# One adaLN block on one core: condition and beta loaded as single rows and spread by TensorE, and half of the second segment's LayerNorm statistics moved to an earlier place

## The chip, the cores and the metric

The kernel runs on one core of one Trainium2 chip. The metric is the device time of one execution in microseconds (us), the median of several executions. The engines are TensorE (PE in the profile, with its weight loads as PEld), VectorE (DVE), ScalarE (ACT), GpSimd (POOL) and SyncE (SP), which issues nearly all DMAs here.

## The reference

The block is a conditioned transformer layer on x of 2048 rows by 512 columns, all in float32. Six vectors of 512 come from a condition vector `c` of 512. The attention half runs over four segments of 512 rows with 32 heads of 16 columns; each segment attends within itself, and a compressed memory `M`, `z` carries what came before. A gate per head, `g = sigmoid(beta)`, mixes the two. The second half is a bilinear feed-forward part of 1376 columns.

```python
mod = (_silu(c) @ w_mod).reshape(c.shape[0], 6, 1, -1)
sa, ca, ga, sb, cb, gb = (mod[:, 0], mod[:, 1], mod[:, 2], mod[:, 3], mod[:, 4], mod[:, 5])
h = _layernorm(x, axis=-1) * (1 + ca) + sa
x = x + ga * _A_ref(h, A_wq, A_wk, A_wv, A_wo, A_beta)
h = _layernorm(x, axis=-1) * (1 + cb) + sb
x = x + gb * _B_ref(h, B_w_gate, B_w_up, B_w_down)
...
o = g * a_mem + (1.0 - g) * a_dot
M = M + jnp.einsum("bhld,bhle->bhde", pk, vs)
```

## The kernel before, in words

**The opening.** The kernel first needs two of the six vectors, `sa` and `ca`, as columns. SP's queue issues the loads in this order: four tiles of `x` for segment 0 (128 x 512 each), the first half of the needed columns of `w_mod` (tiles `wm`, four loads of 256 KB), the first weights of k (`wrk`), the second half of `wm`, the weights of q (`wrq`) and of v (`wrv`), and then those of k and q for the heads' groups 1 and 2. ScalarE's queue issues two small loads: `c` as a tile `s_c` of 128 partitions x 4 (L628), and `beta` sent to all 128 partitions as `be`, 128 x 32 (L669). While these travel, TensorE multiplies a tile of zeros (`wu`) 18 times (L658, `NWU = 18`, output `wups`, never read).

From `s_c` ScalarE and VectorE make silu(c): `e1 = exp(-c)`, plus one, reciprocal, product (L670 to L673). TensorE then multiplies by the first half of `wm` (`mod0(0)`, tile `m` in the profile). VectorE meanwhile takes mean and variance of the four tiles of `x` (`bn_stats` and `bn_aggr`, tiles `ast` and `amv`) and normalises them; TensorE transposes them (tiles `atp`), multiplies by the second half of `wm` (`mod0(1)`, whose first operand, `r0[1][1]`, is prepared by ScalarE and VectorE), and goes on to the projections k, q (`kps`, `qps`) and v (`vps`). VectorE's and ScalarE's work here is held in the order of the text by two chains, `CV` and `CA`; TensorE's by `pe()`.

**The gates.** `gates()` (L677 to L690) turns `be` into `gg` (from `exp(-beta)`) and `omg` (from `exp(beta)`): one VectorE step on each, a copy of `omg` into the eight `v` tiles by GpSimd, then the two reciprocals on VectorE, and products with a mask `hmg` on GpSimd.

**The loop.** 32 units follow (four segments, four groups of eight heads, two halves), each with five slots. In each slot the code, written out by hand, places the products for the row maxima (`q_half`: TensorE product `q<-kst,qst`, then VectorE's maximum over it, one custom instruction that reads PSUM and a short one that reads out `nm`), the logits and exponentials (`k_step`), and the sums over v (`av_step`). Between them `fill()` hands out pieces of the other work from a generator `fill_a`: projections of the next groups, the memory's steps, and the LayerNorm of the next segment (`ln`, which yields after each tile's statistics). `weave(a, b, at)` lets pieces of `b` follow the pieces of `a` whose numbers stand in `at`. For segment 1 the loads of `x` (`xload`, L643) and the LayerNorm begin in `fill_a` at segment 0, group 2: its four statistics go into the pieces 0, 1, 2, 3 of `Q`, the projection of q.

**Staging.** `staged()` hands out the tiles that raw weights are loaded into; four of them have the tag `x`, that is, they use the same four buffers as the tiles of `x`.

Of the kernel before, what the change touches and what calls it, by code (L numbers as in the profile page):

```python
# [57 lines left out]
def tile_kernel(ctx, tc, x, wq, wk_, wv, wo, beta, w_gate, w_up, w_down, c, w_mod, out):  # L58
# [113 lines left out]
    def ln(pool, hpool, xt, s, sc, sh, pfx, hb, fast):  # L172

        first = pfx == "a" and s == 0
        V, A = (CV, CA) if first else (vec, act)
        mv = pool.tile([P, 4, 2], F32, tag="mv", name=f"{pfx}mv{s}", bufs=2)
        for t in range(4):
            st = pool.tile([P, 6], F32, tag="st", name=f"{pfx}st{s}_{t}", bufs=2)
            i = V.bn_stats(st, xt[t])
            if not first:  # L180
                pin(i)
            V.bn_aggr(mv[:, t, :], st)
            if not first:
                yield 0.0
        sd = pool.tile([P, 4], F32, tag="sd", name=f"{pfx}sd{s}", bufs=2)
        A.activation(sd, mv[:, :, 1], AF.Ln, bias=epst[:, 0:1])
        y = pool.tile([P, 4], F32, tag="y", name=f"{pfx}y{s}", bufs=2)
        A.activation(y, sd, AF.Exp, scale=-0.5)
        a = pool.tile([P, 4], F32, tag="ya", name=f"{pfx}ya{s}", bufs=2)
        b = pool.tile([P, 4], F32, tag="yb", name=f"{pfx}yb{s}", bufs=2)  # L190
        eng = CV if first else nc.gpsimd
        eng.tensor_mul(a, y, y)
        if first:
            CV.scalar_tensor_tensor(b, mv[:, :, 1], EPS, a, op0=ALU.add, op1=ALU.mult)
        else:
            eng.tensor_scalar(b, mv[:, :, 1], 1.0, EPS, op0=ALU.mult, op1=ALU.add)
            eng.tensor_mul(b, b, a)
        eng.tensor_scalar(b, b, -0.5, 1.5, op0=ALU.mult, op1=ALU.add)
        eng.tensor_mul(y, y, b)
        yield 0.0  # L200
        tps = [bank(f"{pfx}tp{s}_{d}") for d in range(KT)] if first else []
        for t in range(4):
            i = V.tensor_scalar(xt[t], xt[t], mv[:, t, 0:1], y[:, t:t + 1],
                                op0=ALU.subtract, op1=ALU.mult)
            if not first:
                pin(i)
                yield 0.0
            for d, ps in enumerate(tps):
                TP(ps[:, t * P:(t + 1) * P], xt[t][:, d * P:(d + 1) * P], ident)
        if first:  # L210
            yield 0.0
        hH, hL = [], []
        if first:
            hcur[0] = hH, hL
        for d in range(KT):
            if first:
                ps = tps[d]
            else:
                ps = bank(f"{pfx}tp{s}_{d}", small=pfx == "c" and s == 0)
                for t in range(4):  # L220
                    TP(ps[:, t * P:(t + 1) * P], xt[t][:, d * P:(d + 1) * P], ident)
            h = pool.tile([P, L], F32, tag="hf", name=f"{pfx}hf{s}_{d}", bufs=hb[2])
            A.activation(h, ps, AF.Identity, scale=sc[:, d:d + 1], bias=sh[:, d:d + 1])
            hi = hpool.tile([P, L], F32R, tag=hb[0].format(d), name=f"{pfx}hH{s}_{d}", bufs=hb[1])
            lo = hpool.tile([P, L], F32R, tag=hb[0].format(4 + d), name=f"{pfx}hL{s}_{d}", bufs=hb[1])
            if fast:
                if d % 2:
                    A.activation(hi, h, AF.Copy)
                else:
                    V.tensor_copy(hi, h)  # L230
                V.tensor_sub(lo, h, hi.bitcast(F32))
# [393 lines left out]

    pwpool, pw = open_pool(name="pw", bufs=1, reuse_waits="tile")
    papool, pa = open_pool(name="pa", bufs=2, reuse_waits="tile")
    nc.scalar.dma_start(s_c, c)  # L628
    wm = w_mod.rearrange("(k p) n -> p k n", p=P)

    def load_mod(i):
# [13 lines left out]
        return xt  # L645

    xts = {0: xload(0)}
    NWU = 18
    wu = pa.tile([P, 512], BF, tag="rl", name="wu", bufs=1)
    vec.memset(wu, 0.0)  # L650
    wups = psp.tile([P, 2, 512], F32, tag="lk", name="wups", bufs=1)
# [2 lines left out]
        for i in range(n):  # L654
            MM(wups[:, 0], wu[:, 0:P], wu, start=True, stop=True)

    warm(NWU)
    wm0 = []  # L658
    for k in range(KT):
        a = ap.tile([P, 2, 2, 256], F32, tag="pt", name=f"wm0_{k}", bufs=PT)  # L660
# [5 lines left out]

    wm0_load(0)
    r0 = [[a[:, j].rearrange("p i c -> p (i c)") for a in wm0] for j in range(2)]
    nc.scalar.dma_start(be, beta[None, :].to_broadcast([P, H]))  # L669
    act.activation(e1, s_c, AF.Exp, scale=-1.0)  # L670
    CV.tensor_scalar_add(e1, e1, 1.0)
    CV.reciprocal(e1, e1)
    scl = CV.tensor_mul(s_c, s_c, e1)  # L673
    for a in kst:
        tc.add_manual_dep(nc.gpsimd.memset(a[96:98].rearrange("p h t -> p (h t)").bitcast(F32), ONES2).ins, scl.ins.name, SYNC, reason="order")

    def gates():  # L677

        CA.activation(gg, be, AF.Exp, scale=-1.0)
        act.activation(omg, be, AF.Exp)  # L680
        CV.tensor_scalar(omg, omg, 1e30, 1.0, op0=ALU.min, op1=ALU.add)
        for a in vt[0] + vt[1]:
            nc.gpsimd.tensor_copy(a[:, 0:H * VS].rearrange("p (h e) -> p h e", e=VS)[:, :, DH], omg)
        CV.tensor_scalar_add(gg, gg, 1.0)
        for tl in (gg, omg):
            CV.reciprocal(tl, tl)
        for g in range(NG):
            nc.gpsimd.tensor_mul(hmg[:, g, :, 0:DH], hmg[:, g, :, 0:DH],
                                 gg[:, g * HG:(g + 1) * HG].unsqueeze(2).to_broadcast([P, HG, DH]))
            nc.gpsimd.tensor_mul(hmg[:, g, :, DH], hmg[:, g, :, DH], omg[:, g * HG:(g + 1) * HG])  # L690
# [51 lines left out]
                i += 1  # L742

    wH, wL = {}, {}
    stage = [("ph", 3), ("ph", 3), ("ph", 3), ("mem", 1), ("pkr", 1), ("f", 2)] + [("x", 4)] * 4 + [("mem", 1), ("memb", 2)]
    nst = [0]

    def staged(nm):
        tg, n = stage[nst[0] % len(stage)]
        nst[0] += 1  # L750
        return (ap if tg == "memb" else pa).tile([P, D], F32, tag=tg, name=f"wr{nm}", bufs=n)

    def load_g(nm, w, g):
# [223 lines left out]
    def fill_a():  # L977
# [1 line left out]
            next(w)  # L979
        yield from av  # L980
        memq.extend((a_mem(0, 0), a_mem(0, 1)))
        lns = None
        for s in range(NSEG):
            if s > 0:
                hcur[0] = yield from lns
# [2 lines left out]
            for g in range(2 if s == 0 else 0, NG):  # L988
# [7 lines left out]
                    B["orl"] = wo_load(0, wpool)  # L996
                if g >= 2 and s + 1 < NSEG:
                    if g == 2:
                        xts[s + 1] = xload(s + 1)
                        lns = a_ln(s + 1)  # L1000
                        Q = weave(Q, lns, (0, 1, 2, 3))
                    else:
                        K = weave(K, lns, (1,) if s > 0 else (0, 1, 3))
                        Q = weave(Q, lns, (0, 1, 2, 3) if s > 0 else (0, 1))
# [125 lines left out]
    w1 = [load_g(nm, w, 1) for nm, w in (("k", wk_), ("q", wq))]  # L1130
    for w in w1:
        next(w)
    run(kq0[1])
    run(kq0[0])
    load(0)
# [4 lines left out]
        next(w)  # L1140
    for i in range(3):
        next(av)
    gates()
    w2 = [load_g(nm, w, 2) for nm, w in (("k", wk_), ("q", wq))]
    for w in w2:
# [536 lines left out]
```

## Time and profile before

| | |
|---|---|
| median of three runs | 854.2 us (853.75 to 854.21) |
| the profiled execution's own time | 854.15 us |
| its span, first to last instruction | 852.4 us |
| PE busy | 835.3 us, 98% of the span |
| DVE busy | 643.1 us, 75% |
| ACT busy | 499.0 us, 59% |
| POOL busy | 276.8 us, 32% |
| granted TensorE clock of the run | 1.0 |

All times in the text count from the span's start. A row of the timeline has the start, the time, the engine, the line, the operation, the tiles (output before the arrow), the shapes and a count; in brackets stands the engine's idle time before it and what the profile infers to have ended it. Rows of one engine with the same line and tiles that follow each other are merged, with a count. VectorE's operations through the chain `CV` all have line L39, and TensorE's through its helper L85 or L88, so they are told apart by their tiles.

### The profile page before, as it was taken

Reading aid. Unit: us, or ns where it says so; the run is one execution under the profiler, and the core shown is the slowest. Engines: PE = TensorE matmul, PEld = TensorE weight load, DVE = VectorE, ACT = ScalarE, POOL = GpSimd, SP = SyncE. Lnnn points to the kernel's source line nnn. Section 1 sums busy time; section 2 is a strip of 40 time slices with the busy share of each in tenths; the row PEclk is TensorE's granted clock in tenths of the full one; section 3 lists DMA queues with packets and bytes.
Section 4 is the critical chain, followed back from the end, with each engine's and each line's share of the span. In section 5 each row is a group of like instructions: output and inputs, shape, how many; then the busy total and the mean of one; then the engine's idle time right before and its main releaser. Section 6 shows DMA issues by size and latency. Waiting matters only on the chain.

```text
span 852.4 us, 14404 instructions
## 1 busy us (share of the span) xinstructions
PE 835.3 (98%) x4972; PEld 597.4 (70%) x4972; DVE 643.1 (75%) x1797; ACT 499.0 (59%) x760; POOL 276.8 (32%) x423
## 2 busy tenths in 40 slices
PE   9989999999999999999999999999999999999998
PEld 6756656666665656666665687888888778888886
DVE  7897768887778967787888359989987855447654
ACT  4758767787676876677545626344435555555330
POOL 2756627566565774675434610000000000000000
PEclk9999999999999999999999999999999999999999
DMA  9645435563545554466675466587650685335102
GB/s 271 155 152 155 121 104 141 158 179 115 143 106 166 144 165 106 122 170 213 195 216 155 145 192 230 189 287 271 253 201 28 234 271 210 121 135 184 43 8 98
DMA packets 83928, 139.57 MB, mean 164 GB/s; under 512 B 12720, under 2 KB 46768, under 8 KB 83856
## 3 DMA queue, kind: packets, MB, share of 16 engines
q1 hardware_dynamic: 83424, 138.51, 52.0%
q8 instruction: 39, 0.64, 0.3%
q14 instruction: 33, 0.27, 0.1%
q10 hardware_dynamic: 432, 0.15, 0.1%
HBM read 89.87 MB, written 48.50 MB: 162 GB/s over the span
## 4 chain that ended last, share of the span: by engine, by line
PE 61%; DVE 5%; ACT 1%; issue 0%; POOL 0%; DVEq 0%
PE acc L1358 14%; PE Xg L1289 7%; PE Xu L1289 6%; PE wops L85 5%; PE tb L85 5%; PE Yu L1289 4%; PE Yg L1289 4%; PE k L85 3%; PE q L85 3%; DVE q L39 2%; PE Zg L1289 1%; PE Zu L1289 1%; PE qps L85 1%; PE vps L85 1%; PE Xx L1289 1%; PE up L85 1%
## 5 line engine op out<-in xcount | busy, mean ns | idle before, releaser
L39 DVE CUSTOM_DVE_ANT_0 q<-q,cmask 128x384 f32<-128x384 f32 (+3 forms) x512 | 248.2, 503 | 71.1 <-PE q L85 63.5
L335 ACT ACTIVATE pt<-k 128x1024 f32<-128x1024 f32 x160 | 164.0, 1025 | 74.2 <-PE k L85 71.4
L341 POOL TENSOR_SCALAR_AFFINE_SELECT pt<-pt 128x256 f32<-128x256 f32 (+1 forms) x224 | 98.0, 452 | 137.2 <-ACT pt L335 136.9
L85 PE MATMUL q<-kst,qst 96*128 96x384 bf16 (+3 forms) x512 | 122.8, 302 | 6.5 <-DVE nm L39 5.1
L85 PE MATMUL k<-qst,kst 98*128 98x384 bf16 (+3 forms) x512 | 96.0, 299 | 1.6 <-ACT pt L335 1.3
L1366 DVE TENSOR_TENSOR xa<-xa,acc 128x512 f32<-128x512 f32 x95 | 64.9, 684 | 39.6 <-PE acc L1358 37.8
L85 PEld LDWEIGHTS <-qst 96*128 96x128 bf16 x512 | 43.9, 98 | 58.4 <-issue 43.6
L85 PE MATMUL tb<-pt,v 128*32 128x512 f32 (+3 forms) x1024 | 75.5, 436 | 0.0
L39 DVE DVE_READ_ACCUMULATOR2_ANT nm<- 128x1 f32 x512 | 71.8, 140 | 0.0
L85 PEld LDWEIGHTS <-kst 98*128 98x128 bf16 x512 | 44.4, 98 | 24.9 <-issue 8.8
L1358 PE MATMUL acc<-dH,mH 128*128 128x512 f32 (+1 forms) x152 | 60.3, 397 | 0.0
L1358 PE MATMUL acc<-dL,mH 128*128 128x512 f32 (+1 forms) x152 | 60.1, 395 | 0.0
L1358 PE MATMUL acc<-dH,mL 128*128 128x512 f32 (+1 forms) x152 | 60.0, 395 | 0.0
L85 PEld LDWEIGHTS tb<-pt,v 128*32 128x32 f32 x1024 | 28.7, 109 | 38.6 <-issue 35.7
L367 ACT ACTIVATE tsb<-tb 128x512 f32<-128x512 f32 x32 | 19.1, 596 | 31.6 <-PE tb L85 31.5
L1358 PEld LDWEIGHTS acc<-dH,mL 128*128 128x128 f32 (+1 forms) x152 | 28.5, 188 | 7.1 <-DVE mL L1309 0.3
L1358 PEld LDWEIGHTS acc<-dL,mH 128*128 128x128 f32 (+1 forms) x152 | 28.6, 188 | 7.0
L1358 PEld LDWEIGHTS acc<-dH,mH 128*128 128x128 f32 (+1 forms) x152 | 28.5, 188 | 6.8
L85 PE MATMUL kps<-ahH,wkH 128*128 128x512 f32 x64 | 29.4, 460 | 0.0
L85 PE MATMUL qps<-ahH,wqH 128*128 128x512 f32 x64 | 28.7, 448 | 0.2 <-DVE oL L39 0.2
L85 PE MATMUL vps<-wvH,ahH 128*128 128x512 f32 x64 | 28.3, 442 | 0.0
L85 PE MATMUL wops<-woH,oH 128*128 128x512 f32 x64 | 28.3, 442 | 0.0
(403 smaller groups left out, 2019.1 us busy)
## 6 DMA issues: line engine op xcount, KB each, us to landing
wm<-in_w_mod_dram SPq DMA_DIRECT2D x24, 256.0 KB, 3.9
kd<-k SPq DMA_DIRECT2D x16, 384.0 KB, 2.5
qd<-q SPq DMA_DIRECT2D x16, 384.0 KB, 3.5
kst<-kd SPq DMA_DIRECT2D x32, 192.0 KB, 3.2
qst<-qd SPq DMA_DIRECT2D x32, 192.0 KB, 3.7
x<-in_x_dram SPq DMA_DIRECT2D x16, 256.0 KB, 4.8
kst<-kd SPq DMA_DIRECT2D x32, 128.0 KB, 3.2
qst<-qd SPq DMA_DIRECT2D x32, 128.0 KB, 3.7
```

The costliest lines, as they stand in the source:

```text
L39: i = getattr(self.eng, name)(*a, **k)
L85: return pe(nc.tensor.matmul(*a, **k))
L335: ex = act.activation(pt, kp, AF.Exp, scale=0.25)
L341: sels[u, i] = nc.gpsimd.affine_select(w, w, pattern=[[0, w.shape[1]], [1, P]], compare_op=ALU.is_ge, fill=0.0, base=0, channel_multiplier=-1)
L367: act.activation(tsbs[u], tbs.pop(u), AF.Copy)
L1289: pe(nc.tensor.matmul(ps[0:n], a, b[:, k], start=first and c == 0, stop=last and c == 5, skip_group_check=True))
L1358: pe(nc.tensor.matmul(ps, a[0:m, t * P:(t + 1) * P], b[0:m], start=j == 0, stop=j == n - 1))
L1366: vec.tensor_add(xa, xa, ps)
```

## The change

`c` and `beta` are loaded as one row each, into one partition (`crow`, 1 x 512, and `brow`, 1 x 32). Five small products on TensorE spread them over the partitions, into the second half of the `wups` tile: four of 128 x 1 for `c`, one of 128 x 32 for `beta`. They stand after three products of zeros; seven more follow, so there are 10 in place of 18. ScalarE reads `e1` and `be` from there, VectorE `s_c`. The steps on `e1` move, on VectorE, behind the statistics of the first tile of `x`.

The loads of segment 1's `x` are issued in the opening, and the raw weights that used the buffers of the tag `x` take those of the tag `pt`. Segment 1's LayerNorm is created before `gates()`, and two of its four statistics are taken there, one after each reciprocal; the other two are woven into the pieces 0 and 3 of `Q`.

```diff
@@ ln
             V.bn_aggr(mv[:, t, :], st)
+            if first and t == 0:
+                condition()
@@
-    nc.scalar.dma_start(s_c, c)
+    crow = pa.tile([P, D], F32, tag="mem", name="crow", bufs=1)[0:1]
+    brow = pa.tile([P, D], F32, tag="pkr", name="brow", bufs=1)[0:1, 0:H]
+    nc.scalar.dma_start(crow, c)
+    nc.scalar.dma_start(brow, beta[None, :])
@@
-    NWU = 18
...
-    warm(NWU)
+    warm(3)
+    cps = wups[:, 1, 0:KT]
+    for k in range(KT):
+        MM(cps[:, k:k + 1], crow[:, k * P:(k + 1) * P], ones[0:1, 0:1], start=k == 0, stop=k == KT - 1, skip_group_check=True)
+    bps = wups[:, 1, KT:KT + H]
+    MM(bps, ones[0:1, :], brow, start=True, stop=True, skip_group_check=True)
+    warm(7)
@@
-    nc.scalar.dma_start(be, beta[None, :].to_broadcast([P, H]))
-    act.activation(e1, s_c, AF.Exp, scale=-1.0)
-    CV.tensor_scalar_add(e1, e1, 1.0)
-    CV.reciprocal(e1, e1)
-    scl = CV.tensor_mul(s_c, s_c, e1)
...
+    act.activation(e1, cps, AF.Exp, scale=-1.0)
+    act.activation(be, bps, AF.Copy)
+
+    def condition():
+
+        CV.tensor_scalar_add(e1, e1, 1.0)
+        CV.reciprocal(e1, e1)
+        scl = CV.tensor_mul(s_c, cps, e1)
...
@@ gates
+        vec.eng = CV
         for tl in (gg, omg):
             CV.reciprocal(tl, tl)
+            next(ln1)
@@
-    stage = [("ph", 3), ("ph", 3), ("ph", 3), ("mem", 1), ("pkr", 1), ("f", 2)] + [("x", 4)] * 4 + [("mem", 1), ("memb", 2)]
+    stage = [("ph", 3), ("ph", 3), ("ph", 3), ("mem", 1), ("pkr", 1), ("f", 2)] + [("pt", PT)] * 4 + [("mem", 1), ("memb", 2)]
@@ fill_a
-        lns = None
+        lns = ln1
...
-                        xts[s + 1] = xload(s + 1)
-                        lns = a_ln(s + 1)
-                        Q = weave(Q, lns, (0, 1, 2, 3))
+                        if s > 0:
+                            xts[s + 1] = xload(s + 1)
+                            lns = a_ln(s + 1)
+                        Q = weave(Q, lns, (0, 1, 2, 3) if s > 0 else (0, 3))
@@
     for w in w1:
         next(w)
+    xts[1] = xload(1)
...
+    ln1 = a_ln(1)
     gates()
@@ kernel
-    vals[9] = vals[9].reshape(KT, P).T
+    vals[9] = vals[9].reshape(1, D)
```

Three places in the order of the instructions show what moves. The first is VectorE at the gates, before the change (`phk` is a feature map of k, and `q` with `nm` the first row maximum of the loop):

```order
L39 TENSOR_SCALAR gg<-gg 128x32
L39 RECIPROCAL gg<-gg 128x32
L39 RECIPROCAL omg<-omg 128x32
L853 SCALAR_TENSOR_TENSOR phk_1_539<-phk_1_539,rlk_1_540 128x512
L39 ISA q_0_0_590,nm_589<-q_0_0_590,cmask 128x512
```

and with it:

```order
L39 TENSOR_SCALAR gg<-gg 128x32
L39 RECIPROCAL gg<-gg 128x32
L39 BN_STATS ast_0_512<-x_0_435 128x6
L39 BN_AGGR amv_511<-ast_0_512 128x2
L39 RECIPROCAL omg<-omg 128x32
L39 BN_STATS ast_1_516<-x_1_437 128x6
L39 BN_AGGR amv_511<-ast_1_516 128x2
L39 SCALAR_TENSOR_TENSOR phk_1_554<-phk_1_554,rlk_1_555 128x512
L39 ISA q_0_0_605,nm_604<-q_0_0_605,cmask 128x512
```

Two tiles' statistics now stand around the second reciprocal, ahead of the loop's first row maximum. The second place is VectorE in the loop, in segment 0, where the projection of q for group 2 is woven in; before the change:

```order
L39 BN_STATS ast_0_747<-x_0_635 128x6
L39 BN_AGGR amv_746<-ast_0_747 128x2
L39 BN_STATS ast_1_753<-x_1_637 128x6
L39 BN_AGGR amv_746<-ast_1_753 128x2
L39 ISA q_2_1_759,nm_683<-q_2_1_759,cmask 128x512
L39 ISA nm_683 128x1
L39 SCALAR_TENSOR_TENSOR phk_2_723<-phk_2_723,rlk_2_724 128x512
L39 ISA q_3_0_763,nm_683<-q_3_0_763,cmask 128x384
L39 ISA nm_683 128x1
L39 ISA q_3_0_763,nm_683<-q_3_0_763,cmask 128x128
L39 ISA nm_683 128x1
L39 BN_STATS ast_2_775<-x_2_639 128x6
```

and with it:

```order
L39 BN_STATS ast_2_753<-x_2_439 128x6
L39 BN_AGGR amv_511<-ast_2_753 128x2
L39 ISA q_2_1_762,nm_690<-q_2_1_762,cmask 128x512
L39 ISA nm_690 128x1
L39 SCALAR_TENSOR_TENSOR phk_2_730<-phk_2_730,rlk_2_731 128x512
L39 ISA q_3_0_766,nm_690<-q_3_0_766,cmask 128x384
L39 ISA nm_690 128x1
L39 ISA q_3_0_766,nm_690<-q_3_0_766,cmask 128x128
L39 ISA nm_690 128x1
L39 ISA q_3_1_787,nm_690<-q_3_1_787,cmask 128x384
```

One pair of statistics is gone ahead of the maximum of `q_2_1`, and one ahead of the first maximum of `q_3_1`; the fourth tile's statistics stay where they were. The third place is SP's queue in the opening, with the change:

```order
L791 DMA wrv_269<-in_wv_dram 128x512
L776 DMA wrk_427<-in_wk_dram 128x4x128
L776 DMA wrq_431<-in_wq_dram 128x4x128
L648 DMA x_0_435<-in_x_dram 128x512
L648 DMA x_1_437<-in_x_dram 128x512
L648 DMA x_2_439<-in_x_dram 128x512
L648 DMA x_3_441<-in_x_dram 128x512
L776 DMA wrk_527<-in_wk_dram 128x4x128
L776 DMA wrq_531<-in_wq_dram 128x4x128
L847 DMA kd_0_107<-k_0_0_420 128x3x512
```

Before the change the four loads of `x` were not here: the second `wrk` followed the first `wrq` directly, and the loads of `x` stood behind the weights of group 3, around the writes of `kd_1` and `qd_1` to memory. TensorE's order is the same in both kernels from the first product `m` on.

More of the change, by code (lines that the diff above doesn't have):

```diff
@@ L668, in tile_kernel @@
     r0 = [[a[:, j].rearrange("p i c -> p (i c)") for a in wm0] for j in range(2)]
-    nc.scalar.dma_start(be, beta[None, :].to_broadcast([P, H]))
-    act.activation(e1, s_c, AF.Exp, scale=-1.0)
-    CV.tensor_scalar_add(e1, e1, 1.0)
-    CV.reciprocal(e1, e1)
-    scl = CV.tensor_mul(s_c, s_c, e1)
-    for a in kst:
-        tc.add_manual_dep(nc.gpsimd.memset(a[96:98].rearrange("p h t -> p (h t)").bitcast(F32), ONES2).ins, scl.ins.name, SYNC, reason="order")
+    act.activation(e1, cps, AF.Exp, scale=-1.0)
[4 more added lines that the diff above has]
+        scl = CV.tensor_mul(s_c, cps, e1)
+        for a in kst:
+            tc.add_manual_dep(nc.gpsimd.memset(a[96:98].rearrange("p h t -> p (h t)").bitcast(F32), ONES2).ins, scl.ins.name, SYNC, reason="order")
     def gates():
@@ L750, in staged @@
         nst[0] += 1
+        if tg == "pt":
+            return ap.tile([P, 2, 512], F32, tag=tg, name=f"wr{nm}", bufs=n)[:, 0]
         return (ap if tg == "memb" else pa).tile([P, D], F32, tag=tg, name=f"wr{nm}", bufs=n)
```

## The prediction

> **What bounds the kernel now.** I read the page's first part, then tables of stretches, then the timeline where TensorE waits. The page says that TensorE is busy for nearly the whole span:
>
> ```profile
> PE 835.3 (98%) x4972; PEld 597.4 (70%) x4972; DVE 643.1 (75%) x1797; ACT 499.0 (59%) x760; POOL 276.8 (32%) x423
> ```
>
> So time can only be won where TensorE idles, where its work goes, or where it starts sooner. The table of stretches (columns: us, busy time and instructions of PE, PEld, DVE, ACT, POOL, clock, DMA share, GB/s) shows where it idles early on:
>
> ```profile
> 40.00:50.00 10.00, 8.86 (x51) 6.24 (x49) 9.07 (x36) 4.99 (x8) 5.54 (x5) 1.00 0.51 161
> 50.00:60.00 10.00, 8.45 (x49) 5.54 (x48) 9.69 (x37) 6.30 (x11) 5.62 (x6) 1.00 0.52 152
> ```
>
> From 40 to 60 us VectorE is the bound (9.07 and 9.69 of 10 us) and TensorE idles for 1.1 and 1.55 us. The other place is the opening, where TensorE does nothing useful before 8.79 us:
>
> ```profile
> 1.69 6.82 PE L85 MATMUL wups<-wu 128*128 128x512 bf16 x18 [1.69 <-DVE wu L650]
> 6.79 0.15 PEld L85 LDWEIGHTS <-wu 128*128 128x128 bf16 x1 [0.28 <-issue]
> 7.21 0.80 PEld L85 LDWEIGHTS <-wu 128*128 128x128 bf16 x4 [0.28 <-issue]
> 8.79 3.78 PE L85 MATMUL m<-s_c,wm 128*128 128x96 f32 x32 [0.27 <-DVE ast L39]
> 12.41 1.91 PE L88 MATMUL atp<-ident,x 128*128 128x128 f32 x16
> 14.27 1.13 PE L85 MATMUL m<-ones,wm 128*128 128x96 f32 x8
> 16.97 0.48 PE L85 MATMUL kps<-ahH,wkH 128*128 128x512 f32 x1
> ```
>
> From 8.79 on there is no idle time ahead of TensorE's rows up to the first product of k, `kps`, so the opening's gain is how much sooner `m` starts, if nothing behind it comes late. What `m` waited for is not `ast`: the first `wm` was issued at 2.67 and landed 6.0 us later at the soonest, at 8.67.
>
> ```profile
> 2.67 2.38 SPq L665 DMA_DIRECT2D wm<-in_w_mod_dram  x4
> DMA to landing us min/median/max: 6.0/6.2/6.8
> ```
>
> **Term 1, the loop.** Two of four statistics leave the stretch where VectorE is the bound. Their rows before:
>
> ```profile
> 52.01 0.66 DVE L39 BATCH_NORM_STATS2 ast<-x 128x6 f32<-128x512 f32 x1
> 52.80 0.67 DVE L39 CUSTOM_DVE_ANT_0 q<-q,cmask 128x512 f32<-128x512 f32 x1
> 54.87 0.69 DVE L39 BATCH_NORM_STATS2 ast<-x 128x6 f32<-128x512 f32 x1
> 55.69 0.54 DVE L39 CUSTOM_DVE_ANT_0 q<-q,cmask 128x384 f32<-128x384 f32 x1
> PE q L85 <- DVE nm L39: 1.6, 4, 0.7
> ```
>
> From each statistic to the next maximum pass 0.79 and 0.82 us, 1.61 together. The last row, of the waits from 50 to 65 us, says that TensorE waits 1.6 us there for VectorE's maxima. So at most 1.6 us come free; at least about 0.8, if TensorE's own work then binds after the first pair. VectorE is busy for 9.69 of the 10 us from 50 to 60, so I stay near the top: **1.45 us**.
>
> Where they go, VectorE idles:
>
> ```profile
> 30.92 0.35 DVE L39 RECIPROCAL gg<-gg 128x32 f32<-128x32 f32 x1
> 32.20 0.35 DVE L39 RECIPROCAL omg<-omg 128x32 f32<-128x32 f32 x1 [0.92 <-POOL v L683]
> 33.57 3.80 DVE L853 SCALAR_TENSOR_TENSOR phk<-phk,rlk 128x512 f32<-128x512 f32 x1 [1.02 <-ACT phk L848]
> 55.06 1.15 POOL L825 TENSOR_TENSOR qr<-qf,q 128x512 f32<-128x512 f32 x1
> 38.10 0.38 PE L85 MATMUL q<-kst,qst 96*128 96x384 bf16 x2 [0.19 <-DVE nm L39]
> ```
>
> A statistic of 0.82 fits into 0.92 and into 1.02 us, with 0.1 and 0.2 to spare. GpSimd is busy there, and the `phk` row shows that it can stretch a VectorE instruction from under 0.7 to 3.80 us; but the statistic at 54.87 took 0.69 beside GpSimd's product at 55.06, so I cost this at nothing. Without that cover, 1.6 us would be late ahead of the loop's first maxima, for which TensorE waits already (38.10), and term 1 would be gone.
>
> The four loads of `x` move past `kd_1` and `qd_1` on SP's queue, which frees these, and stand ahead of the weights of group 2:
>
> ```profile
> 15.78 0.61 SPq L759 DMA_DIRECT2D wrq<-in_wq_dram  x1
> wrq<-in_wq_dram SPq DMA_DIRECT2D x3, 256.0 KB, 7.1
> 28.90 1.27 ACT L764 ACTIVATE wkH<-wrk 128x512 fp32r<-128x512 f32 x1
> 54.67 1.00 ACT L335 ACTIVATE pt<-k 128x1024 f32<-128x1024 f32 x1
> 58.13 0.38 SPq L830 DMA_DIRECT2D qd<-q  x1
> 64.03 1.76 SPq L274 DMA_DIRECT2D qst<-qd  x3
> ```
>
> The last of those weights is issued at 15.78 and, with 7.1 us, lands at 22.9, 6 us before ScalarE takes the first up at 28.90. A megabyte at 387 GB/s (below) makes them 2.7 us later: nothing. The staging buffers of the tag `pt` need no wait on the transposes: nothing either. ScalarE now takes an exponential of 1.00 us ahead of the conversion of q for group 2, and GpSimd a mask ahead of its part; q's write to memory, at 58.13, may come 1 us later, and is read back from 64.03: nothing.
>
> **Term 2, the opening.** The loads stall early (same columns as above):
>
> ```profile
> 2.00:3.20 1.20, 1.20 (x4) 0.45 (x3) 0.77 (x4) 0.09 (x1) 0.27 (x1) 1.00 1.04 237
> 3.20:5.60 2.40, 2.40 (x7) 0.85 (x6) 1.30 (x5) 0.20 (x1) 0.96 (x2) 1.00 0.38 108
> 6.40:8.00 1.60, 1.60 (x7) 0.69 (x6) 1.04 (x4) 0.23 (x1) 1.60 (x3) 1.00 1.06 387
> 1.27 0.45 ACTq L669 DMA_DIRECT2D be<-in_beta_dram  x1
> 3.70 0.20 ACT L670 ACTIVATE e<-s_c 128x4 f32<-128x4 f32 x1 [1.61 <-DMA s_c<-in_c_dram]
> s_c<-in_c_dram ACTq DMA_DIRECT2D x1, 2.0 KB, 2.8
> be<-in_beta_dram ACTq DMA_DIRECT2D x1, 16.0 KB, 5.2
> ```
>
> From 3.2 to 5.6 us only 108 GB/s move, with the engines 0.38 busy; before and after, 237 and 387. In that stretch `be` is under way: issued at 1.27, 16 KB, landed 5.2 later at 6.5, while `s_c` took 2.8. I take the 128 small copies of one row as the cause, for that coincidence alone. At 387 GB/s, 2.4 us would move 0.67 MB more, **1.7 us** of loads, and all that is queued behind comes that much sooner: the first `wm` at about 7.0. Bounds: 0 if `be` is not the cause, 1.7 if it is.
>
> Then the shorter warm-up decides. Three products at 0.43 (the steps between the 6.79 and 7.21 rows) end near 3.0. `crow`, taken as quick as `s_c`, is there at 3.7, and `brow`, issued at 1.27, with the same 2.8 at 4.1. TensorE now waits for both with the warm-ups and `m` queued behind. Five tiny products and seven of 0.43 give 4.25 + 3.0 = 7.3 for the start of `m`, 1.45 sooner than 8.79. What follows keeps up:
>
> ```profile
> 5.84 0.69 DVE L39 BATCH_NORM_STATS2 ast<-x 128x6 f32<-128x512 f32 x1 [0.50 <-DMA x<-in_x_dram]
> 8.77 0.18 DVE L39 BATCH_NORM_AGGREGATE amv<-ast 128x2 f32<-128x6 f32 x1
> 10.35 1.91 DVE L39 TENSOR_SCALAR x<-x,amv,ay 128x512 f32<-128x512 f32 x4
> 12.58 0.72 ACT L39 ACTIVATE wm<-wm,s_c 128x512 f32<-128x512 f32 x1 [3.06 <-DMA wm<-in_w_mod_dram]
> 13.46 0.75 DVE L39 SCALAR_TENSOR_TENSOR wm<-wm,s_c,wm 128x512 f32<-128x512 f32 x1 [0.63 <-DMA wm<-in_w_mod_dram]
> ```
>
> The first statistic fits before silu(c), for which ScalarE and VectorE now wait on TensorE's tiny products, and whose steps then end near 5.0; three more of 0.9 end near 7.7 in place of 8.95, so normalising runs from about 9.1 to 11.0, and the transposes, due at 10.95, find their tiles. The second half of `wm` waits for DMA at 12.58 and 13.46; 1.7 sooner, its product is ready by 12.4, and TensorE wants it at 12.85.
>
> The clock is the doubt. The first 13 warm-ups step at 0.43 us and the last at about 0.22, though the table's clock column reads 1.00 throughout: the array runs at half rate until 7.2, 5.5 us after it began. Now there is a pause from 3.0 to 4.2. Counted from the first product, full rate still comes at 7.2 and nothing is lost; counted from 4.25 it comes at 9.75, and `m` loses (9.75 - 7.3) / 2 = 1.2. The trace cannot choose between the two; I take the middle, 0.6 lost. Term 2 is 1.45 - 0.6, rounded to **0.8 us**, with 0.2 to 1.45 as its ends and 0 without the DMA's gain.
>
> [...]
>
> **The sum.** The profiled execution took 854.15 us, which agrees with the median of 854.2. 854.15 - 1.45 - 0.8 = **851.9 us**.
>
> **Rivals.**
> 1. TensorE reaches full rate before `m`: it starts at 7.0 to 7.3 and loses nothing. 854.15 - 1.45 - 1.6 = 851.1. For it speaks that seven warm-ups nearly touch `m`; against it, the pause.
> 2. The change doesn't do what its loads are for: `be` was not what held the loads. `m` still starts at 8.7, TensorE pauses 1.3 us instead of warming, and only the loop counts: 852.7. For it: a coincidence is all I have.
> 3. The loop's gain is taken by another wait: with VectorE earlier, TensorE waits for ScalarE's exponentials or GpSimd's part of the LayerNorm instead. Only 0.2 of term 1 is left: 854.15 - 0.2 - 0.8 = 853.1. Against it: no such wait of weight stands in that stretch.
> 4. Slower, by the clock: the loads come no sooner, TensorE idles from 7.3 to 8.7, the count starts again, and the opening's products run at half rate to 16 us. They lose (16 - 8.79) / 2 = 3.6: 854.15 + 3.6 - 1.45 = 856.3. It decides the sign once half rate lasts beyond 8.79 + 2 x 1.45 = 11.7, and is measurably slower beyond 15.1.
>
> **How the numbers follow.** A measurement of this kernel can tell about 0.2%, 1.7 us, from no change, so faster means below 852.45 and slower above 855.85. The forecast gets 0.40, rival 1 0.17, rival 2 0.20, rival 3 0.13, rival 4 0.10. The forecast's own ends, 1.0 to 3.05 us of gain, put 0.35 of its 0.40 below 852.45; with rival 1, and 0.03 of rivals 2 and 3, faster has 0.55, slower 0.10, same 0.35. The range goes from both terms at their best, 854.15 - 1.6 - 1.7 = 850.8, a little lower for the timing of `brow`, 850.5, up past rival 3 to a mild case of rival 4, 854.0.
>
> **What would show it.** Right: `be`'s stretch from 3.2 to 5.6 us moves over 300 GB/s; `m` starts near 7.3; the first `kps` at 16.2 in place of 16.97; two statistics between the reciprocals without stretching them; TensorE's waits for `nm` from 50 to 65 us below 0.4. Wrong: `m` still at 8.7, or `m`'s 32 products taking well over 3.78 us; statistics that last over 0.8 us at the gates; new waits on `pt` or GpSimd near 55 us.

## The result, and the profile after

The changed kernel is slower. Its median is 856.24 us (855.1 to 857.42, 11 runs), that of the kernel before, measured beside it, 853.88 us (852.63 to 855.03, 11 runs); the ratio is 1.0025, with a 95% interval of 1.0016 to 1.0034. That is 2.4 us, a quarter of a percent, more; 851.9 was predicted, and 856.24 lies above the range's upper end of 854.0. The profiled execution of the changed kernel took 855.10 us (span 853.4), 0.95 more than that of before.

The timeline of TensorE in the opening shows the first loss (start, time, engine, line, operation, tiles, shapes, count, and in brackets the idle time before):

```profile
3.08 1.86 PE L85 MATMUL wups<-ones,crow 1*128 1x1 f32 x8
4.81 0.61 PE L85 MATMUL wups<-brow,ones 1*128 1x32 f32 x2
5.35 3.17 PE L85 MATMUL wups<-wu 128*128 128x512 bf16 x7
9.50 3.81 PE L85 MATMUL m<-s_c,wm 128*128 128x96 f32 x32 [0.98 <-DVE s_c L39]
14.14 1.94 PE L88 MATMUL atp<-ident,x 128*128 128x128 f32 x16 [0.83 <-DVE x L39]
18.92 0.48 PE L85 MATMUL kps<-ahH,wkH 128*128 128x512 f32 x1
```

`m` starts at 9.50 instead of 8.79, and waits for `s_c`, not for a load. `kps` stands at 18.92 instead of 16.97, 1.95 us late. What `s_c` waited for is on ScalarE and VectorE, in the same timeline:

```profile
8.55 0.17 ACT L679 ACTIVATE e<-wups 128x4 f32<-128x4 f32 x1 [6.45 <-PE wups L85]
9.28 0.16 DVE L39 TENSOR_TENSOR s_c<-wups,e 128x4 f32<-128x4 f32 x1
9.36 0.68 DVE L39 BATCH_NORM_STATS2 ast<-x 128x6 f32<-128x512 f32 x1
13.45 1.91 DVE L39 TENSOR_SCALAR x<-x,amv,ay 128x512 f32<-128x512 f32 x4
```

The products that spread `crow` and `brow` are done at 5.42, yet the exponential waits until 8.55, just behind the end of the last warm-up (5.35 + 3.17 = 8.52). The spread columns lie in the second half of the tile `wups`, into whose first half the seven later warm-ups write. The chain `CV` then holds the statistics of the other three tiles of `x` behind `s_c`, so normalising starts at 13.45 instead of 10.35, and the transposes `atp` wait for it.

The table of stretches (columns as in the prediction) shows the loads and the loop:

```profile
3.20:5.60 2.40, 2.40 (x11) 2.21 (x12) 0.88 (x2) 0.00 (x0) 0.00 (x0) 1.00 0.95 315
50.00:60.00 10.00, 9.40 (x55) 6.23 (x54) 9.69 (x39) 7.17 (x12) 5.95 (x7) 1.00 0.49 120
```

From 3.2 to 5.6 us 315 GB/s move instead of 108. From 50 to 60 us TensorE is busy for 9.40 us instead of 8.45. From 60 to 70 us something comes back: it is busy for 9.10 instead of 9.76.

To see how far TensorE stands behind the kernel before at a given point, take the same product in both. Three that are easy to find are two transposes `ntp` and the products `tb`; first the kernel before, then the changed one:

```profile
47.36 0.27 PE L88 MATMUL ntp<-ident,nm 128*16 128x128 f32 x1
59.36 0.27 PE L88 MATMUL ntp<-ident,nm 128*16 128x128 f32 x1
67.00 2.36 PE L85 MATMUL tb<-pt,v 128*32 128x512 f32 x32
```

```profile
49.01 0.27 PE L88 MATMUL ntp<-ident,nm 128*16 128x128 f32 x1
59.46 0.27 PE L88 MATMUL ntp<-ident,nm 128*16 128x128 f32 x1
68.06 2.36 PE L85 MATMUL tb<-pt,v 128*32 128x512 f32 x32
```

The changed kernel is 1.65 us late at the first, 0.10 at the second and 1.06 at the third. The loop wins 1.55 us, about what term 1 promised, and then gives 0.96 back. Rows of VectorE and GpSimd show where, first VectorE before the change, then both engines after it:

```profile
62.48 0.55 DVE L39 TENSOR_SCALAR x<-x,amv,ay 128x512 f32<-128x512 f32 x1 [0.40 <-POOL ay L199]
64.46 0.54 DVE L39 TENSOR_SCALAR x<-x,amv,ay 128x512 f32<-128x512 f32 x1
```

```profile
59.53 1.17 POOL L846 TENSOR_TENSOR q<-qr,q 128x512 bf16<-128x512 f32 x1
62.60 0.20 POOL L201 TENSOR_TENSOR ay<-ay,ayb 128x4 f32<-128x4 f32 x1
62.83 0.55 DVE L39 TENSOR_SCALAR x<-x,amv,ay 128x512 f32<-128x512 f32 x1 [0.65 <-POOL ay L201]
64.69 1.16 POOL L842 TENSOR_TENSOR kr<-kf,k 128x512 f32<-128x512 f32 x1 [0.69 <-ACT k L841]
64.81 1.32 DVE L39 TENSOR_SCALAR x<-x,amv,ay 128x512 f32<-128x512 f32 x1
```

VectorE waits 0.65 us, with the maxima queued behind it, for `ay`, the last of GpSimd's small operations, which stand behind its conversion of q. In the kernel before that wait is 0.40, so it costs 0.25 us more. The next normalising starts 0.12 us after GpSimd's product `kr` and takes 1.32 us instead of 0.54; by the next `tb` the rest of the 0.96, 0.71 us, is gone.

Behind `tb` the distance changes at two more places. From 366 to 376 us the changed kernel falls another 0.73 us behind. GpSimd waits there for a load of `wor`, a raw weight of the output projection; the kernel before first:

```profile
363.65 1.29 POOL L957 TENSOR_TENSOR wor<-wor,gab 128x512 f32<-128x512 f32 x1 [0.54 <-DMA wor<-in_wo_dram]
```

```profile
365.82 1.28 POOL L974 TENSOR_TENSOR wor<-wor,gab 128x512 f32<-128x512 f32 x1 [1.73 <-DMA wor<-in_wo_dram]
```

The load landed 3.9 us after its issue instead of 2.7, and behind it TensorE waits 0.31 us ahead of a `tb` and 0.39 ahead of an `up`. The 13 profiles of kernels that spread rows (the changed kernel's seven and those of e1, e2, e4, e5, e7 and e8 below) all have these two waits, the other five have neither. So this loss belongs to the rows; no run shows how they bring it about. From 516 to 520 us the changed kernel wins 0.77 us, but only because this execution of the kernel before waits 0.60 us there for VectorE's `mL`. That wait comes and goes from execution to execution, whatever the kernel (0.61 us in e15, none in e10).

### The profile page after: what moved, and what is told of

The parts are those of the page before. It is cut to its first block, busy times and chain, and to the rows that moved or that the text cites. A ratio compares the mean times of both kernels' runs of the same rounds, so it can differ in the third digit from the quotient of the medians.

```text
span 853.4 us, 14415 instructions
## 1 busy us (share of the span) xinstructions
PE 835.2 (98%) x4974; PEld 598.2 (70%) x4974; DVE 641.5 (75%) x1797; ACT 498.1 (58%) x761; POOL 275.5 (32%) x423
## 4 chain that ended last, share of the span: by engine, by line
PE 59%; DVE 5%; ACT 2%; DMA 1%; SPq 1%; issue 1%; POOL 1%; DVEq 0%
PE acc L1378 14%; PE Xg L1309 6%; PE Xu L1309 6%; PE wops L85 5%; PE tb L85 4%; PE Yu L1309 4%; PE Yg L1309 4%; PE k L85 3%; PE q L85 3%; DVE q L39 2%; PE Zg L1309 1%; PE Zu L1309 1%; PE qps L85 1%; PE vps L85 1%; DMA crd<-in_w_down_dram 1%
## 5 line engine op out<-in xcount | busy, mean ns | idle before, releaser
L85 PE MATMUL q<-kst,qst 96*128 96x384 bf16 (+3 forms) x512 | 122.7, 302 | 5.7 <-DVE nm L39 5.1
L85 PE MATMUL k<-qst,kst 98*128 98x384 bf16 (+3 forms) x512 | 96.0, 299 | 1.6 <-ACT pt L337 1.3
L85 PEld LDWEIGHTS <-qst 96*128 96x128 bf16 x512 | 43.9, 98 | 57.3 <-issue 42.7
L85 PE MATMUL tb<-pt,v 128*32 128x512 f32 (+3 forms) x1024 | 75.7, 436 | 0.3 <-POOL pt L343 0.3
L85 PEld LDWEIGHTS <-kst 98*128 98x128 bf16 x512 | 44.5, 98 | 25.2 <-issue 9.2
L85 PEld LDWEIGHTS tb<-pt,v 128*32 128x32 f32 x1024 | 28.6, 109 | 39.2 <-issue 35.4
L85 PE MATMUL kps<-ahH,wkH 128*128 128x512 f32 x64 | 29.5, 460 | 0.0
L85 PE MATMUL qps<-ahH,wqH 128*128 128x512 f32 x64 | 28.7, 449 | 0.0
L85 PE MATMUL wops<-woH,oH 128*128 128x512 f32 x64 | 28.3, 442 | 0.0
L85 PE MATMUL vps<-wvH,ahH 128*128 128x512 f32 x64 | 28.3, 442 | 0.0
```

The lines of the kernel that those rows point to most:

```text
L85: return pe(nc.tensor.matmul(*a, **k))
```

## The experiments

Each run was timed beside the kernel before on the same chip. "Late" and "ahead" are the same product's start against the profile of before, as above. The first four test the opening: theory T is the shared tile, rival C the clock.

### e1: a PSUM tile of its own for the spread columns

```diff
-    cps = wups[:, 1, 0:KT]
+    spr = pst((P, 512), "sm", "spr")
+    cps = spr[:, 0:KT]
-    bps = wups[:, 1, KT:KT + H]
+    bps = spr[:, KT:KT + H]
```

> The whole change, but the five spreading products write a PSUM tile of their own instead of the second half of the warm-ups' tile. Theory T (a shared tile): in the changed kernel ScalarE's exponential of the condition starts at 8.55 us because it waits for the last of the warm-ups, which write the same tile, and behind it stand silu(c), the statistics of three tiles of x and the first product m. Then here that exponential starts near 5.0, s_c is ready by 5.8, m starts at about 8.5 when the warm-ups end, the first kps at 16.3 to 16.8 in place of 18.92, and the time is 1.0 to 1.3 us under the kernel before (near 852.7). Rival C (the clock): the loss comes from TensorE at half rate during m; then the exponential is early but the time stays 1.5 us or more above the kernel before (855.5 or more).

Measured: 853.1 us (852.36 to 854.58, 11 runs) against 853.6 for before; ratio 0.9995 (0.9986 to 1.0004). Its profiled execution:

```profile
5.35 2.98 PE L85 MATMUL wups<-wu 128*128 128x512 bf16 x7
5.46 0.17 ACT L680 ACTIVATE e<-spr 128x4 f32<-128x4 f32 x1 [3.36 <-PE spr L85]
8.17 3.71 PE L85 MATMUL m<-s_c,wm 128*128 128x96 f32 x32
10.35 1.91 DVE L39 TENSOR_SCALAR x<-x,amv,ay 128x512 f32<-128x512 f32 x4
16.06 0.48 PE L85 MATMUL kps<-ahH,wkH 128*128 128x512 f32 x1
46.35 0.27 PE L88 MATMUL ntp<-ident,nm 128*16 128x128 f32 x1
56.78 0.27 PE L88 MATMUL ntp<-ident,nm 128*16 128x128 f32 x1
65.39 2.36 PE L85 MATMUL tb<-pt,v 128*32 128x512 f32 x32
```

The exponential runs at 5.46, 0.04 us behind the end of the small products (4.81 + 0.61 = 5.42), with nothing else changed: `kps` comes 2.86 us sooner than in the changed kernel and 0.91 sooner than before, and the median falls by 3.1 us. The wait was for the tile, not for what was read. Even here the exponential waits for the products of `brow`, which write the same tile: those of `crow`, which it reads, end at 4.94 (3.08 + 1.86). Against the kernel before the median falls by 0.5 us only, where 1.0 to 1.3 were expected, and its interval includes no change; the loss at 366 to 376 us, 0.53 here, is a part of that. The loop again wins 1.57 us (from 1.01 ahead to 2.58) and gives 0.97 back (1.61).

### e2: the condition's steps behind all four statistics

```diff
-            if first and t == 0:
+            if first and t == 3:
                 condition()
```

> The whole change, with silu(c) on VectorE behind all four statistics of x rather than behind the first. Theory T: m still starts at 9.5, but the statistics are done by 7.5 us and no longer queue behind the wait, so the tiles are normalised from about 10.3 instead of 13.45, the transposes follow m at once, and the first kps comes near 18.0 instead of 18.92: about 0.9 us under the change as it stands, still some 1.3 us above the kernel before. Rival C: nothing of weight hangs on the order on VectorE, and the time is that of the change, 2.4 us above the kernel before.

Measured: 856.6 us (853.9 to 857.09, 9 runs); ratio 1.0025 (1.0016 to 1.0035). The profile was of an execution in which `m` ran long:

```profile
9.50 5.99 PE L85 MATMUL m<-s_c,wm 128*128 128x96 f32 x32 [0.98 <-DVE s_c L39]
10.78 3.74 DVE L39 TENSOR_SCALAR x<-x,amv,ay 128x512 f32<-128x512 f32 x4
```

Normalising starts 2.67 us sooner than in the changed kernel, but `m` takes 5.99 us instead of 3.81, and `kps` comes at 19.67, where 18.0 was expected. The normalising itself takes 3.74 us instead of 1.91, beside GpSimd's filling of `kst` (9.57 to 13.78), which waits for `s_c`. In the median nothing is won, but two of the nine runs, 853.9 and 854.29 us, lie below the changed kernel's fastest, 855.1. So the run does not settle the order of VectorE's work; it points at TensorE's rate during `m` as a second cause.

### e3 and e4: one half of the change each

e3 is the kernel before with the statistics, the loads of `x` and the staging alone; e4 is the changed kernel without them, that is, the two rows alone. The core of what e3 adds and e4 takes away:

```diff
+        vec.eng = CV
         for tl in (gg, omg):
             CV.reciprocal(tl, tl)
+            next(ln1)
...
-                        Q = weave(Q, lns, (0, 1, 2, 3))
+                        Q = weave(Q, lns, (0, 1, 2, 3) if s > 0 else (0, 3))
```

> The kernel before with only the second half of the change: segment 1's x loaded in the opening, two of its statistics between the gates' reciprocals, the raw weights in the other buffers. Theory T: the opening is that of the kernel before, and the loop wins what the trace of the change shows, about 0.9 us net (1.6 won by 59 us, 0.7 given back to a wait for GpSimd's part of the LayerNorm): near 853.0. Rival: the prediction's term, 1.45 us, near 852.4; or nothing, 853.9.

> The kernel before with only the first half of the change: condition and beta as rows, spread by TensorE, warm-ups 3 and 7. Theory T: the opening ends 2 us later, as in the trace of the change (kps at 18.9 instead of 16.97), and nothing is won in the loop: near 856. Rival C: 857 or more, with the products m taking well over 3.8 us in the trace. Together with the run that has only the statistics it shows whether the two halves add up to the 2.4 us of the whole.

e3 took 853.33 us (852.32 to 854.93, 11 runs), ratio 0.9995 (0.9986 to 1.0004); e4 took 856.11 (855.73 to 857.26, 7 runs), ratio 1.003 (1.0019 to 1.0041). The rows alone are the whole loss; the statistics alone are worth next to nothing in the median (0.3 us, where 0.9 was expected). The profiled execution of e4, 857.26 us, had a long `m` too: 5.92 us, with `kps` at 19.59. e3's rows show the loop's win and give-back without any trouble in the opening:

```profile
47.53 0.27 PE L88 MATMUL ntp<-ident,nm 128*16 128x128 f32 x1
57.97 0.27 PE L88 MATMUL ntp<-ident,nm 128*16 128x128 f32 x1
61.34 0.55 DVE L39 TENSOR_SCALAR x<-x,amv,ay 128x512 f32<-128x512 f32 x1 [0.65 <-POOL ay L199]
63.32 1.31 DVE L39 TENSOR_SCALAR x<-x,amv,ay 128x512 f32<-128x512 f32 x1
66.57 2.36 PE L85 MATMUL tb<-pt,v 128*32 128x512 f32 x32
```

It goes from 0.17 late to 1.39 ahead, then to 0.43 ahead: 1.56 won, 0.96 given back, with the same wait of 0.65 and the same 1.31 as in the changed kernel.

### e10: the clock by itself

```diff
-    NWU = 18
+    NWU = 4
```

> The kernel before with 4 warm-ups in place of 18: TensorE pauses from about 3.4 us to the start of m near 8.7. [...] Rival (the clock depends on time since the start or on TensorE's work as a whole, not on a pause): m at 3.8, kps near 17, no change.

Measured: 855.69 us (854.68 to 856.5, 8 runs) against 853.46; ratio 1.0024 (1.0013 to 1.0034).

```profile
8.75 7.12 PE L85 MATMUL m<-s_c,wm 128*128 128x96 f32 x32 [5.17 <-DVE ast L39]
20.20 0.48 PE L85 MATMUL kps<-ahH,wkH 128*128 128x512 f32 x1
```

`m` takes 7.12 us, 3.34 more than in the kernel before, with the same loads and the same start. The steps between its products are 0.21 us to the end, against 0.11 in the kernel before, so all of `m` runs at half rate; the steps of the transposes behind it fall from 0.21 to 0.11 at about 16.0, so half rate lasted for about 7.3 us from the start of `m`. `kps` comes 3.2 us late, the median rises by 2.2. Theory K (a pause puts off the full rate) stands for a pause of 5.17 us, and the rival falls.

### e5: zeros in TensorE's pause

```diff
     warm(7)
+    wub = pst((P, 512), "sm", "wub")
+    for i in range(3):
+        MM(wub, wu[:, 0:P], wu, start=True, stop=True)
```

> The changed kernel with three more products of zeros behind the seven, into a PSUM tile of their own, so that TensorE is busy in the pause of about 1 us between its last warm-up (8.52 us) and the first product of m (9.50 us); nothing else waits for them. Theory K (the pause sometimes puts off full rate to about 14 us, and this is why the changed kernel's median stands 1.1 us above its profiled execution): the switch comes near 8.5 in every execution, m's 32 products take 3.8 us, kps stays near 18.9, the profile stays near 855.1, and the median falls to it, 0.5 to 1.2 us below the changed kernel's 856.24, with a narrower spread. Rival (the spread has another cause): median still near 856.2, and m in the profile as often 5.9 us as 3.8.

Measured: 855.29 us (854.56 to 856.83, 12 runs) against 853.63; ratio 1.0021 (1.0012 to 1.0029). In the profile, 854.73 us, nothing idles ahead of `m`, `m` took 3.96 us and `kps` came at 18.92. The median fell as expected, by 0.95 us, but the interval overlaps that of the changed kernel, and the spread did not shrink. Inconclusive by itself.

### e11 to e16: six more profiles of the changed kernel

> The changed kernel, one more execution with its profile. Theory K: if the time is near 855.1, m's 32 products take 3.8 us and kps comes near 18.9; if it is from 856 to 857.4, m takes 5 to 6 us and kps comes at 19.6 or later, with the loop as in the first profile. Rival: a time over 856 with m at 3.8 us.

> The changed kernel, a third execution with its profile, for the same question: theory K says that a time over 856 goes with m at 5 to 6 us and kps at 19.6 or later, one near 855.1 with m at 3.8; the rival, that the time differs with m at 3.8.

> The changed kernel, a fourth execution with its profile. Theory K: a time over 856 goes with m's 32 products at 5 to 6 us and kps at 19.6 or later, one near 855.1 with m at 3.8 us. Rival: the time differs with m at 3.8 us in each.

> The changed kernel, a fifth execution with its profile: as for the fourth.

> The changed kernel, a sixth execution with its profile: as for the fourth.

> The changed kernel, a seventh execution with its profile: as for the fourth.

With the first profile this makes seven:

| execution | time, us | `m`'s 32 products, us | `kps` at |
|---|---|---|---|
| first profile | 855.10 | 3.81 | 18.92 |
| e11 | 855.24 | 3.81 | 18.73 |
| e12 | 855.14 | 3.81 | 18.91 |
| e13 | 856.71 | 5.64 | 19.32 |
| e14 | 856.74 | 6.98 | 20.66 |
| e15 | 855.75 | 3.81 | 18.91 |
| e16 | 855.18 | 3.81 | 18.92 |

The rows of e14 show it best; `m` starts at the same time and after the same pause as in the first profile, and only its rate differs:

```profile
9.50 6.98 PE L85 MATMUL m<-s_c,wm 128*128 128x96 f32 x32 [0.98 <-DVE s_c L39]
20.66 0.48 PE L85 MATMUL kps<-ahH,wkH 128*128 128x512 f32 x1
```

Both executions over 856 us have the long `m`, and no other has. In e14 the later `kps` (1.74 us) is all of the difference to the first profile (1.64). In e13 it is 0.4 of 1.6, and e15 is 0.65 above the first with the same opening. The rest of both lies mainly between 516 and 520 us, at the wait for `mL`: 0.95 us in e13, 0.60 in e15. So theory K accounts for e14, but not for most of e13. How often the long `m` comes in the 11 timed runs is not known.

### e6: the broadcast of beta late

The kernel before, with this alone; SP issues the load behind those of group 1's weights:

```diff
-    NWU = 18
+    NWU = 14
...
-    nc.scalar.dma_start(be, beta[None, :].to_broadcast([P, H]))
...
+    pin(nc.sync.dma_start(be, beta[None, :].to_broadcast([P, H])))
```

> The kernel before with nothing of the change but a test of its ground: the broadcast of beta to 128 partitions is issued on SP's queue behind the loads of the opening instead of on ScalarE's at 1.27 us, and 14 warm-ups stand in place of 18. Theory D (that broadcast holds up the loads next to it): 3.2 to 5.6 us move over 300 GB/s, the tiles of x land near 3.5, 4.2, 5.1, 6.0 in place of 3.5, 5.8, 7.2, 7.9, the first wm near 7.2 in place of 8.65, m starts near 7.7 at the end of the warm-ups, kps 15.6 to 16.1 in place of 16.97; about 0.9 to 1.3 us faster than before, 852.6 median. Rival (the loads stall at that time whatever beta does): loads land as before, m at 8.7, kps 17, no gain.

Measured: 852.52 us (852.23 to 853.3, 11 runs) against 853.63; ratio 0.9987 (0.9978 to 0.9995).

The row of the table of stretches, and the timeline:

```profile
3.20:5.60 2.40, 2.40 (x9) 0.93 (x8) 1.41 (x6) 0.20 (x1) 0.81 (x1) 1.00 0.99 339
```

```profile
7.48 3.78 PE L85 MATMUL m<-s_c,wm 128*128 128x96 f32 x32 [1.11 <-DMA wm<-in_w_mod_dram]
15.61 0.48 PE L85 MATMUL kps<-ahH,wkH 128*128 128x512 f32 x1
```

339 GB/s in place of 108, the first product of `m` 1.31 us sooner, `kps` 1.36 us sooner. Theory D stands: the broadcast of one row to 128 partitions held the loads. The fewer warm-ups are not the cause: e10 has four of them and the broadcast in its old place, and its `m` starts at 8.75. `m` keeps full rate (3.78 us) across a pause of 1.11 us.

### e7 and e8: GpSimd's small operations

e7 has the own tile of e1, and takes the last two statistics together, earlier, so that `ay` is made ahead of q's conversion. e8 has the own tile, and VectorE makes `ay`.

```diff
-                        Q = weave(Q, lns, (0, 1, 2, 3) if s > 0 else (0, 3))
+                        Q = weave(Q, lns, (0, 1, 2, 3) if s > 0 else (0, 1, 2))
...
-                        K = weave(K, lns, (1,) if s > 0 else (0, 1, 3))
+                        K = weave(K, lns, (1,) if s > 0 else (1, 3))
```

```diff
-        eng = CV if first else nc.gpsimd
+        eng = CV if first else vec if pfx == "a" and s == 1 else nc.gpsimd
```

> The changed kernel with the PSUM tile of its own for condition and beta, and with the last two statistics of segment 1 in the pieces 0 and 1 of Q instead of 0 and 3, so that GpSimd's five small operations on ay come ahead of its conversion of q. Theory G (after the loop's gain of 1.6 us about 1 us is given back because the first normalising waits 0.65 us for GpSimd's ay and the next is stretched to 1.32 us by GpSimd's kr): the wait for ay goes, and from TensorE's lead of 2.6 us at 59 us at least 2.0 are kept at 68 instead of 1.6; 0.3 to 0.6 us below the kernel with its own tile alone (853.1). Rival (the gain meets another wait, whatever GpSimd does, or two statistics in a row cost as much at 52 us as is won): lead at 68 us still 1.6 or less, 853.1 or more.

> The changed kernel with the PSUM tile of its own, and the five small operations on ay of segment 1 taken by VectorE instead of GpSimd. Theory G: the first normalising waits for no other engine but has 0.5 to 0.6 us of small operations ahead of it in place of a wait of 0.65; what it wins is little, 0.1 to 0.3 us, unless the next normalising misses GpSimd's kr and falls from 1.32 to 0.55, which would give 0.7 more. Rival: the lead at 68 us is as with the own tile alone, 1.6 us.

e7 took 852.83 us (851.95 to 853.42, 11 runs), ratio 0.9988 (0.9979 to 0.9996); e8 853.4 (852.36 to 854.3, 11 runs), ratio 0.9996 (0.9988 to 1.0005). Rows of e7:

```profile
46.75 0.27 PE L88 MATMUL ntp<-ident,nm 128*16 128x128 f32 x1
58.09 0.27 PE L88 MATMUL ntp<-ident,nm 128*16 128x128 f32 x1
59.80 0.62 DVE L39 TENSOR_SCALAR x<-x,amv,ay 128x512 f32<-128x512 f32 x1
61.86 0.66 DVE L39 TENSOR_SCALAR x<-x,amv,ay 128x512 f32<-128x512 f32 x1
65.17 2.36 PE L85 MATMUL tb<-pt,v 128*32 128x512 f32 x32
```

The wait is gone and the second normalising, which now ends before `kr` starts, takes 0.66 us. From 0.61 ahead it goes to 1.27 and on to 1.83: less is won by 58 us, where two statistics now stand in a row, and nothing is given back. The loop keeps 1.22 us, twice the 0.60 of e1. Theory G stands, though the lead at 68 us was expected at 2.0 and is 1.83, because this execution's opening was 0.4 us behind e1's; the median is 0.3 us below that of e1, the least that was expected, and the two intervals overlap, so theory G rests on the rows. In e8 the five operations are on VectorE's path and the second normalising still meets `kr`:

```profile
60.33 0.16 DVE L39 TENSOR_TENSOR aya<-ay 128x4 f32<-128x4 f32 x1
61.20 0.55 DVE L39 TENSOR_SCALAR x<-x,amv,ay 128x512 f32<-128x512 f32 x1
62.98 1.16 POOL L843 TENSOR_TENSOR kr<-kf,k 128x512 f32<-128x512 f32 x1 [0.61 <-ACT k L842]
63.18 1.24 DVE L39 TENSOR_SCALAR x<-x,amv,ay 128x512 f32<-128x512 f32 x1
```

From 60.33 to 61.20 they cost 0.87 us, and the normalising still takes 1.24. Its lead goes from 1.62 at the second `ntp` to 0.64 at `tb`, so 0.98 is given back with the wait for `ay` gone: the stretched normalising is the larger part. This wins nothing, a little under the 0.1 to 0.3 expected.

### e9: what was found, together

The kernel before with e6's late broadcast and 14 warm-ups, e3's statistics and e7's order; no row is spread by TensorE.

> What has been found, put together: the kernel before with beta's broadcast issued late on SP's queue, 14 warm-ups, the change's two statistics at the gates and early loads of x, and the last two statistics early, so that GpSimd's ay is ready. No products that spread rows. Theories D and G, added up: 1.37 us in the opening (as with the late broadcast alone) and 1.23 in the loop (from -0.60 to -1.83 us in the kernel with early ay) make 854.15 - 2.6 = 851.55 for a profiled execution and, against the median of before, 853.6 - 2.6 = 851.0 or a little more. Rival (the two gains stand for one wait, or the late broadcast meets the early loads of x and takes some back): 852.0 or more.

Measured: 851.32 us (851.14 to 851.98, 11 runs) against 853.46; ratio 0.9976 (0.9967 to 0.9984). It beats both kernels.

```profile
15.70 0.48 PE L85 MATMUL kps<-ahH,wkH 128*128 128x512 f32 x1
64.44 2.36 PE L85 MATMUL tb<-pt,v 128*32 128x512 f32 x32
```

The opening wins 1.27 us (`kps` at 15.70 instead of 16.97), the rest up to `tb` 1.29 more (2.56 ahead at 64.44). In the trace the two gains add up, to 2.56 of the 2.6 us expected; the median is 2.14 us below that of the kernel before.

## Why the prediction was wrong, point by point

1. **The step that failed** is in term 2: the steps of silu(c) "then end near 5.0", and with it `m` at 7.3. It took ScalarE's read to wait for the small products that make its input. The trace after shows that it waits for the last product in the text ahead of it that writes any part of the same tile, the seventh later warm-up (8.55 against that product's end at 8.52), and `s_c` is there at 9.44. e1 shows that this is the cause: another tile for the output, and `s_c`, normalising and `kps` come 2.9 to 3.1 us sooner. What the prediction could have seen: the diff puts the columns into `wups` and `warm(7)` behind them, ahead of the activation, so that the activation's input tile is written seven times more. It had named, as what "ScalarE and VectorE now wait on", the small products only. With this the condition's place on VectorE, ahead of three statistics, became costly: these start at 9.36 instead of about 5.0.
2. **Five "tiny products"** were costed at next to nothing (4.1 to 4.25). They are ten passes in the rows (eight and two) and take 2.34 us (3.08 to 5.42), 0.23 each, though `crow` was there 0.6 us sooner than assumed. Even with a tile of its own, the second warm-ups end at 8.33 in e1, and `m` starts at 8.17, not at 7.3: 0.87 of the 1.45 us that term 2 had for its start. That `kps` comes at 16.06 in e1, close to the forecast 16.2, is in part luck: the 0.6 set aside for the clock was not lost there. e6, which needs no such product, starts `m` at 7.48.
3. **The broadcast as the cause of the stall** was right: 315 GB/s after, 339 in e6 with that part alone. Rival 2 falls.
4. **The clock** was taken as a loss of 0.6, for a pause from 3.0 to 4.2 that did not come: `crow` is there at 3.08, before the third warm-up ends (1.69 + 1.46 = 3.15). What the traces show is a rate, by the steps of the products; the granted clock of every run is 0.999 or 1.0. In five of seven profiles of the changed kernel half rate cost `m` nothing (3.81 us), in two 1.8 and 3.2 us, which put `kps` 0.4 and 1.74 us later. Rival 4 had half rate after a pause, but after another pause: its loads that come no sooner are refuted, and the pause of 0.98 us that is there comes from the late `s_c`. No trace of before shows the 16 us to which it let half rate last; the runs showed 13.3 (e13), 16.2 (e14) and, behind a pause of 5.17 us, 16.0 (e10). The long `m` adds to the loss; it is not its main part. That this pause is what makes `m` long is likely but not shown. Of the nine profiles with it four have an `m` of 5.6 to 7.0 us (e2, e4, e13, e14); the four without it that also spread rows (e1, e5, e7, e8) have 3.71 to 4.40. Without a pause, then, half rate still reaches 1.4 us into `m` in e8. No one length of half rate after a pause comes out of the runs: read from the steps of 0.21 us, it lasted from the start of `m` for about 3.8 (e13), 6.7 (e14) and 7.3 us (e10). In e8 it lasted to about 9.7, 8.0 us after the first product; why, no run shows.
5. **Term 1** was right in size for the place it spoke of: 1.55 us won by 59 us against 1.45 forecast, statistics of 0.64 us at the gates. It missed that 0.96 would be given back within 8 us. Rival 3 named the place, GpSimd's part of the LayerNorm, with 0.2 left over; 0.6 were left. But the wait for it is the smaller part, 0.25; 0.71 is the normalising stretched beside GpSimd's `kr`, which no rival had. e7 gives nothing back with both gone, e8 still 0.98 with the wait alone gone.
6. **Loads of `x` and staging** at nothing: right. From `kps` (1.95 late) to the `ntp` at 47 us (1.65 late) nothing is lost.

For the first profile the sum is then: 1.95 late in the opening, 0.3 won up to 47 us, 1.55 won, 0.96 given back, so 1.06 late at `tb`; then 0.73 lost at 366 to 376 us, and 0.77 won at 516 to 520 by the wait of that execution of the kernel before, so about 1.0, and 0.95 at the end. The median of 11 runs is 2.4 us late. The long `m` and the wait for `mL`, which differ from execution to execution, are a part of what is between; how they are spread over the timed runs is open, and so is what delays the load of `wor`.

## What to carry to other kernels

When an engine reads part of a PSUM tile, look for everything in the text ahead of the read that writes any part of that tile: here dummy products into the other half held the reader until 8.55 us, where with a tile of its own it ran at 5.46 (e1), and the row's `[6.45 <-PE wups L85]` said so at once. A gain on the bound engine in one stretch was kept here only where the helpers that feed its next stretch came sooner too (0.96 of 1.55 us given back in the changed kernel, nothing in e7); follow the lead of one product over another at several points instead of reading one stretch. A broadcast of a short row to 128 partitions is better issued where no load behind it is awaited: in e6 that brought the first product of `m` 1.31 us sooner.

## What the runs showed of the hardware

- One-row products in f32 were not small in the changed kernel: ten passes of 1 x 1 or 1 x 32 took 2.34 us, 0.23 each, beside warm-ups that step at 0.43 us, the half rate.
- With a 16 KB load that repeats one row for 128 partitions under way, 108 GB/s moved from 3.2 to 5.6 us (the kernel before), without it 339 (e6); it made the first weights 1.3 us late (`m` at 8.79 and 7.48).
- The switch to full rate moved from execution to execution with the same instructions: `m` took 3.81, 5.64 and 6.98 us (the changed kernel, e13, e14). A pause of 5.17 us ahead of it cost 3.34 us (e10), one of 1.11 us, behind the switch, nothing (e6), and one of 0.98 us nothing, 1.8 or 3.2 us (the changed kernel). Under warm-ups without a break from 1.69 us on, their step fell from 0.43 to about 0.21 us at 4.65 (e6), 5.93 (e3) and 7.21 (the kernel before), while the clock column reads 1.00 throughout.
- A normalising (f32, SBUF to SBUF) that starts 0.12 us after a GpSimd product took 1.32 us instead of 0.54, and ended at 66.13, 0.28 after that product. In the kernel before the normalising starts 0.13 us ahead of the product; it takes 0.54, and the product 1.43 us instead of 1.16. Both times the later of the two is the one that is stretched; why, no run shows.
